# Rounding of theta and of the second slices of k and q: which engine takes which step

## The chip, the cores and the metric

The kernel runs on one core of a Trainium2 chip. The metric is the device time of one execution in microseconds (us), and the figure for a kernel is the median over its runs. A core has a matrix engine, TensorE (PE in the profile, with PEld for its weight loads), and three engines that matter here beside it: VectorE (DVE), ScalarE (ACT) and the queue of SyncE (SP), which issues the transfers. Each engine works through its own list of instructions strictly in order; an instruction that waits holds up everything behind it on its engine.

## The reference

Two stages in a row. The first is a polysketch attention over 4 batches, 4 heads, 1088 positions and head size 32, with a sketch of r = 8. The second is a token mixer with a phase. The reference is in numpy, float32 for the activations.

```python
def phi(x):                                   # r*r = 64 features of a row
    a = einsum('rd,bhsd->bhsr', S1, x)
    b = einsum('rd,bhsd->bhsr', S2, x)
    return einsum('bhsi,bhsj->bhsij', a, b).reshape(..., r * r)
q_p, k_p = phi(q), phi(k)
kv = einsum('bhsf,bhsd->bhfd', k_p, v)
z = sum(k_p, axis=2)
num = einsum('bhsf,bhfd->bhsd', q_p, kv)
den = einsum('bhsf,bhf->bhs', q_p, z)[..., None] + 1e-06
x = num / den                                 # then (B,H,S,D) -> (B,S,128)

theta = x @ w_theta
zr, zi = x * cos(theta), x * sin(theta)
y = einsum('ts,bsd->btd', w_tok_r, zr) + einsum('ts,bsd->btd', w_tok_i, zi)
u = x + y
return u + maximum(u @ w_ch, 0)
```

The denominator can come close to zero, so the kernel computes `den` far more exactly than float32 allows in one go. It does that by cutting the numbers into slices: a value is rounded to a coarse grid, the rest is rounded to a finer grid, and so on, each slice short enough for exact products in float16 matmuls.

## The kernel before, in words

Positions are padded to 9 chunks of 128. For each batch `b` there are these steps.

- `keys_slices(b)`: k is scaled on ACT into `kx` (128x1152, float32) and cut into three float16 slices in `ks`: slot 1 is the first (coarsest) slice, slot 2 the second, slot 0 the rest. Before the change, slot 2 holds the second slice at 2^12 times its value, and a fourth tile, `half`, holds the same slice at its own scale.
- `query_slices(b)`: q is transposed on PE, scaled on ACT into `qx`, and cut into three float16 slices `sl[0]` to `sl[2]` (tiles q0, q1, q2).
- `matrices(b)`: `keys_sums` multiplies the key slices with each other on PE (lines 306 and 308), `keys_matrix` cuts the sums again into four levels with many small DVE instructions and makes `mv[b]`, the matrix for the denominators.
- `keys_values(b)`: the 64 features of k and their sum with v.
- `features(b)`: 27 float16 matmuls of the query slices with `mv[b]` (lines 446 to 448), copied by ACT into `lv` (line 449).
- `denominators(b)`: some 25 DVE instructions that put `lv` together into the exact reciprocal `rd` of the denominators. They use `fl` (levels put together), `s` (rounded parts), `pr` (products) and `dn` (sums).
- `queries(b, g)` for g = 0, 1, 2 (three chunks each): features of q (`qp`), numerators `num` on PE (line 519), `x` = num times `rd` on DVE, transposes (line 534), theta on PE (line 539), the rounding of theta to whole turns (lines 543 and 544), Abs and two Sin on ACT (lines 545 to 547), and the products `zr`, `zi` on DVE.
- `mixing(b)`: the large part, line 566: 17 slices of `wT` for each of three column groups of up to 384, two PE instructions each, 408 over the four batches; then the channel step and the output (lines 575 to 587).

At the start the token weights arrive as raw float64 bits in 34 pieces. `load_f32` turns each piece into float32 with three ACT instructions (lines 134 to 136) and two DVE instructions (lines 137 and 138).

The order on every engine is not written out by hand: the Tile framework lays it out at build time from priorities and its own cost estimates. The kernel sets five levels of priority, in this order: "first" (all of batch 0 up to its attention), "weights", "out", "attention" (keys and attention of batches 1 to 3) and "mixing". Within a level, earlier code comes first, but a later instruction whose inputs are there may be put into a gap. The program order is: everything of batch 0, `keys(1)`, `attention(1)`, `keys(2)`, `mixing(0)`, `attention(2)`, `keys(3)`, `mixing(1)`, `attention(3)`, `mixing(2)`, `mixing(3)`.

Buffers are shared by tag. Tag `r` has one buffer, used by `big` in `keys_slices`, by `big` in `query_slices` and by `s` in `denominators`. Tag `q2` has one buffer, used by the third query slice and by `half` of the keys. Tag `qx` has one, used by `kx` and `qx`. Tile `tn` is `n_`, tile `tt` is `t_`. The PSUM pool for tag `w` has three buffers, which `features`, `queries`, `query_slices` and `keys_values` share.

The helpers `ts`, `tt` and `stt` issue DVE instructions, with one tensor input and constants (profile line 97), with two tensor inputs (line 93), and with two tensors and a scalar (line 100).

## Time and profile before

| what | value |
|---|---|
| median of 8 runs | 358.92 us (357.41 to 360.18) |
| the profiled execution | 357.59 us |
| its span, first to last instruction | 355.8 us |
| mean granted TensorE clock | 0.882 |
| PE busy | 272.5 us, 77% |
| DVE busy | 250.4 us, 70% |
| ACT busy | 153.5 us, 43% |
| largest group: line 566 on PE, 384 instructions | 135.1 us |

The profile is of one execution. Its first page gives the busy time of each engine, then the span in 40 slices of 8.9 us each with a busy digit for each engine (9 is 90% or more, 0 is under 10%) and the granted clock of TensorE in tenths. Then come the groups of instructions: line, engine, operation, output and input tile, shape, count, then busy time and mean nanoseconds of one, then the idle time of the engine just ahead of them and what ended it. The time line lists instructions in order of start, with their duration and the idle time ahead of them in brackets. The table by stretches gives busy times of all engines and the clock in chosen windows.

### The profile page before, as it was taken

What the parts mean: (1) busy time and instruction counts of PE and PEld (TensorE: products, weight loads), DVE (VectorE), ACT (ScalarE), POOL (GpSimd) and SP (SyncE); (2) the same over time, 40 slices, a digit from 0 to 9 for tenths busy, and PEclk for the clock granted to TensorE, in tenths of its full rate; (3) what the DMA queues carried; (4) which work ended last, traced back from release to release, by engine and by line L of the source; (5) the groups of instructions that cost most, each with busy time, mean ns of one, the idle gap of its engine ahead of it and who ended that gap; (6) DMA issues with size and microseconds to landing.
All of it is one profiled execution on the core that took longest, in us unless ns stands there. A gap on an engine that the chain in (4) does not pass through costs nothing.

```text
span 355.8 us, 4021 instructions
## 1 busy us (share of the span) xinstructions
PE 272.5 (77%) x1355; PEld 191.0 (54%) x1355; DVE 250.4 (70%) x713; ACT 153.5 (43%) x313; POOL 0.7 (0%) x6
## 2 busy tenths in 40 slices
PE   0406580143527999999589999996999999999994
PEld 0304480021425776766267676674777767766662
DVE  4897886977997599569848793996589479532111
ACT  1799729999765451061233513212345131332000
POOL 0000000000000000000000000000000000000000
PEclk9999955558555899999879999997899999999998
DMA  8668537885520012020100222000000000000010
GB/s 298 225 214 277 170 123 254 301 292 171 177 63 3 0 67 68 0 67 3 44 18 2 66 66 90 1 22 20 0 0 3 0 21 3 22 20 0 3 41 18
DMA packets 11604, 28.78 MB, mean 81 GB/s; under 512 B 1216, under 2 KB 5568, under 8 KB 11584
## 3 DMA queue, kind: packets, MB, share of 16 engines
q1 hardware_dynamic: 11376, 28.51, 24.3%
q8 instruction: 10, 0.16, 0.2%
q14 instruction: 10, 0.08, 0.1%
q10 hardware_dynamic: 208, 0.02, 0.0%
HBM read 26.30 MB, written 2.23 MB: 80 GB/s over the span
## 4 chain that ended last, share of the span: by engine, by line
PE 69%; DVE 17%; ACT 10%; DMA 2%; issue 1%; ACTq 0%
PE y L566 37%; PE w L519 4%; PE acc L398 3%; ACT step L135 3%; ACT step L136 3%; PE w L539 2%; PE y L576 2%; PE y L398 2%; DVE wT L93 2%; PE w L513 2%; PE w L388 2%; PE w L446 2%; PE acc L306 2%; DMA s_t_st<-s_t 2%; ACT wT L134 1%; PE w L447 1%
## 5 line engine op out<-in xcount | busy, mean ns | idle before, releaser
L566 PE MATMUL y<-wT,zst 128*128 128x384 f32 (+1 forms) x384 | 135.1, 481 | 1.4 <-DVE zst L93 1.4
L566 PEld LDWEIGHTS y<-wT,zst 128*128 128x128 f32 x384 | 68.2, 193 | 30.8 <-DVE zst L93 2.3
L585 ACT COPY ot<-y 128x384 f32<-128x384 f32 (+2 forms) x16 | 6.0, 399 | 62.0 <-PE y L580 62.0
L135 ACT ACTIVATE step<-st 128x544 f16<-128x544 f32 (+1 forms) x35 | 27.8, 795 | 4.4 <-DVE wT L93 4.3
L93 DVE CUSTOM_DVE_ANT_0 wT<-wT,step 128x1088 uint16<-128x1088 uint16 x34 | 24.3, 714 | 5.8 <-ACT step L136 5.8
L519 PEld LDWEIGHTS w<-kvbd,qpT 128*128 128x128 f32 x144 | 21.6, 213 | 11.0 <-ACT qpT L517 10.0
L136 ACT ACTIVATE step<-st 128x544 int16<-128x544 uint32 (+1 forms) x35 | 27.4, 783 | 0.0
L519 PE MATMUL w<-kvbd,qpT 128*128 128x64 f32 x144 | 23.3, 296 | 3.0 <-ACT qpT L517 2.9
L134 ACT ACTIVATE wT<-st 128x544 f32<-128x544 f32 x34 | 22.9, 683 | 2.0 <-DMA st<-w_tok 2.0
L517 ACT COPY qpT<-w 128x256 f32<-128x256 f32 x36 | 12.8, 368 | 24.8 <-PE w L513 24.8
L513 PE MATMUL w<-ident,qp 128*128 128x128 f32 x72 | 14.6, 304 | 7.8 <-DVE qp L93 7.7
L93 DVE TENSOR_TENSOR uT<-xT,y 128x384 f32<-128x384 f32 (+1 forms) x12 | 6.3, 527 | 19.2 <-PE y L566 19.1
L97 DVE TENSOR_SCALAR tn<-w 128x384 f32<-128x384 f32 x12 | 6.7, 557 | 18.3 <-PE w L539 18.3
L536 ACT COPY xT<-w 128x384 f32<-128x384 f32 x12 | 5.7, 476 | 29.8 <-PE w L534 29.8
L449 ACT COPY lv<-w 128x384 f32<-128x384 f32 x36 | 14.6, 506 | 6.7 <-PE w L448 6.6
L513 PEld LDWEIGHTS w<-ident,qp 128*128 128x128 f32 x72 | 10.1, 170 | 9.6 <-ACT wT L134 7.9
L97 DVE TENSOR_SCALAR wT<-wT 128x544 int32<-128x544 int32 x34 | 14.5, 431 | 0.0
L398 PEld LDWEIGHTS acc<-ld_v,kp 128*128 128x128 f32 x108 | 13.0, 192 | 1.5
L539 PEld LDWEIGHTS w<-w,xT 128*128 128x128 f32 x72 | 10.8, 217 | 5.3 <-ACT xT L536 4.5
L446 PE MATMUL w<-mv,q 128*128 128x384 f16 x36 | 12.6, 351 | 0.8 <-DVE mv L93 0.8
L404 ACT COPY kvbd<-acc 64x64 f32<-64x64 f32 x6 | 1.2, 207 | 27.6 <-PE acc L398 27.6
L539 PE MATMUL w<-w,xT 128*128 128x128 f32 x72 | 12.0, 309 | 1.0 <-ACT xT L536 1.0
(230 smaller groups left out, 511.0 us busy)
## 6 DMA issues: line engine op xcount, KB each, us to landing
st<-w_tok SPq DMA_DIRECT2D x34, 544.0 KB, 4.7
ld_k<-k_l SPq DMA_DIRECT2D x4, 576.0 KB, 3.8
ld_q<-q_l SPq DMA_DIRECT2D x4, 576.0 KB, 4.2
ld_v<-v_l SPq DMA_DIRECT2D x4, 576.0 KB, 4.0
out<-ot SPq DMA_DIRECT2D x8, 192.0 KB, 2.1
out<-ot SPq DMA_DIRECT2D x4, 128.0 KB, 1.8
st<-w_sq SPq DMA_DIRECT2D x1, 256.0 KB, 4.9
out<-ot SPq DMA_DIRECT2D x4, 32.0 KB, 1.8
```

The costliest lines, as they stand in the source:

```text
L93: eng.tensor_tensor(out=o, in0=a, in1=b, op=op)
L97: V.tensor_scalar(out=o, in0=a, scalar1=s1, scalar2=s2, op0=op0, **kw)
L134: A.activation(dst, hi.bitcast(F32), AF.Copy, scale=2.0**-112)
L135: A.activation(step[:, :, 1].bitcast(F16), hi.bitcast(F32), AF.Copy, scale=2.0**-60)
L136: A.activation(step[:, :, 0], lo.bitcast(U32), AF.Copy, scale=2.0**-29)
L398: nc.tensor.matmul(kv[:, n], kp[:, i * H + 2 * n:i * H + 2 * n + 2].rearrange("p h i j -> p (h i j)"), vn[:, c, 2 * n:2 * n + 2].rearrange ...
L446: nc.tensor.matmul(lp, q0, flat[:, 0:4 * W], start=True, stop=False, skip_group_check=True)
L449: A.copy(lv[:, :, :, c].rearrange("p l t n -> p (l t) n"), lp.rearrange("p (x n) -> p x n", n=HR))
L513: nc.tensor.transpose(tr[:, n * P:(n + 1) * P], qp[:, i * H + 2 * n:i * H + 2 * n + 2].rearrange("p h i j -> p (h i j)"), ident)
L519: nc.tensor.matmul(num[:, i * P + n * 2 * D:i * P + (n + 1) * 2 * D], qpT[:, n], kvbd[b][:, n], start=True, stop=True)
L539: nc.tensor.matmul(th[:, i * P:(i + 1) * P], xT[:, i * P:(i + 1) * P], w2[:, 0], start=True, stop=True)
L566: nc.tensor.matmul(yp[:, :t1 - t0], z, wT[:, i, t0:t1], start=(i == 0), stop=(i == NK - 1))
```

## The change

Four edits.

1. In `keys_slices` the second slice is rounded at its own scale (constant 1.5 x 2^23 x 2^-12) straight into slot 2, without `big` and `half`. What is left is found with a plain subtraction, and ACT multiplies it by 2^12 into slot 0. `keys_sums` and `keys_matrix` follow: slot 2 takes the place of `half`, and two factors 2^-12 become 1.
2. In `query_slices` the second slice is rounded at its own scale into a new float16 tile `half`; ACT multiplies it by 2^10 into `sl[1]`; the rest is subtracted, and ACT multiplies it by 2^10 into `sl[2]`. `big` goes.
3. In `denominators` the fourth row of `fl`, which nobody read, goes with its instruction, and two of the three sums in `dn` become one reduction.
4. In `queries` the first half of the rounding of theta (adding the large constant) goes to ACT; DVE then subtracts the constant and theta in one instruction. The sign of the result is turned, so the sine's scale gets a minus.

```diff
@@ keys_slices
-        big = work.tile([P, NC * P], F32, tag="r", name="r", bufs=1)
         ts(ks[:, 1], kx, ROUND, ALU.add, ROUND, ALU.subtract)
         tt(V, kx, kx, ks[:, 1], ALU.subtract)
-        ts(big, kx, 2.0**12, ALU.mult, ROUND, ALU.add)
-        ts(ks[:, 2], big, ROUND, ALU.subtract)
-        stt(ks[:, 0], kx, 2.0**12, ks[:, 2], ALU.mult, ALU.subtract)
-        half = work.tile([P, NC * P], F16, tag="q2", name="half", bufs=1)
-        A.activation(half, ks[:, 2], AF.Copy, scale=2.0**-12)
-        tiles["ks", b] = ks, half
+        ts(ks[:, 2], kx, ROUND * 2.0**-12, ALU.add, ROUND * 2.0**-12, ALU.subtract)
+        tt(V, kx, kx, ks[:, 2], ALU.subtract)
+        A.activation(ks[:, 0], kx, AF.Copy, scale=2.0**12)
+        tiles["ks", b] = ks
@@ keys_sums, keys_matrix
-            nc.tensor.matmul(gp[:, 0:4:3], half[:, cs], ks[:, 0:3:2, cs],
+            nc.tensor.matmul(gp[:, 0:4:3], ks[:, 2, cs], ks[:, 0:3:2, cs],
...
-             [(x[:, 2], 2.0**-12), (x[:, 3], 2.0**-12), (x[:, 0], 2.0**-12)], *SUM, near=2)
+             [(x[:, 2], 1.0), (x[:, 3], 1.0), (x[:, 0], 2.0**-12)], *SUM, near=2)
@@ query_slices
+        half = work.tile([P, NC * P], F16, tag="half", name="half", bufs=1)
...
-        big = work.tile([P, NC * P], F32, tag="r", name="r", bufs=1)
-        ts(big, qx, 2.0**10, ALU.mult, 1.5 * 2.0**22, ALU.add)
-        ts(sl[1], big, 1.5 * 2.0**22, ALU.subtract)
-        stt(sl[2], qx, 2.0**10, sl[1], ALU.mult, ALU.subtract)
+        ts(half, qx, 1.5 * 2.0**12, ALU.add, 1.5 * 2.0**12, ALU.subtract)
+        A.activation(sl[1], half, AF.Copy, scale=2.0**10)
+        tt(V, qx, qx, half, ALU.subtract)
+        A.activation(sl[2], qx, AF.Copy, scale=2.0**10)
@@ denominators
-        fl = work.tile([P, 4, NT], F32, tag="fl", name="fl", bufs=1)
-        stt(fl[:, 0:3], lv[:, 1], 2.0**-10, lv[:, 0], ALU.mult, ALU.add)
+        fl = work.tile([P, 3, NT], F32, tag="fl", name="fl", bufs=1)
+        stt(fl, lv[:, 1], 2.0**-10, lv[:, 0], ALU.mult, ALU.add)
...
-        stt(fl[:, 3], lv[:, 2, 2], 2.0**-20, fl[:, 2], ALU.mult, ALU.add)
...
-        for j, j0, j1 in ((1, 1, 3), (2, 3, 6)):
-            V.tensor_reduce(out=dn[:, j], in_=pr[:, j0:j1].rearrange("p j (n r) -> p n j r", r=R),
-                            axis=AX.XY, op=ALU.add)
+        V.tensor_reduce(out=dn[:, 1], in_=pr[:, 1:6].rearrange("p j (n r) -> p n j r", r=R), axis=AX.XY, op=ALU.add)
...
-        tt(V, dn[:, 0], dn[:, 0], dn[:, 2], ALU.add)
@@ queries
-        ts(n_, th, ROUND, ALU.add, ROUND, ALU.subtract)
-        tt(V, t_, th, n_, ALU.subtract)
+        A.activation(n_, th, AF.Copy, bias=ROUND)
+        stt(t_, n_, ROUND, th, ALU.subtract, ALU.subtract)
         A.activation(n_, t_, AF.Abs)
         A.activation(n_, n_, AF.Sin, bias=halfpi, scale=-TWO_PI)
-        A.activation(t_, t_, AF.Sin, scale=TWO_PI)
+        A.activation(t_, t_, AF.Sin, scale=-TWO_PI)
```

## The prediction

> **What bounds the kernel now.** I read the 40 slices first, then tables by stretches, then the DVE time line where PE stands idle.

> ```profile
> PE   0406580143527999999589999996999999999994
> DVE  4897886977997599569848793996589479532111
> ACT  1799729999765451061233513212345131332000
> PEclk9999955558555899999879999997899999999998
> ```

> Up to slice 12 (113 us) PE is mostly idle, at half clock, while DVE and ACT turn weights into float32 and take batch 0 through its attention. From 113 us on PE is full: 56.75 of 57 us in 113 to 170, 57.61 of 58 in 182 to 240, 91.52 of 92 in 250 to 342. Work taken off DVE or ACT there is worth nothing by itself. Two dents are left, digits 5 and 6:

> ```profile
> 170.00:172.00 2.00, 1.35 (x6) 0.50 (x4) 1.86 (x5) 0.00 (x0) 0.00 (x0) 1.00 0.00 0
> 172.00:174.00 2.00, 0.98 (x3) 0.30 (x2) 2.00 (x4) 0.48 (x1) 0.00 (x0) 1.00 0.22 62
> 174.00:176.00 2.00, 0.55 (x3) 0.31 (x3) 2.00 (x7) 0.48 (x1) 0.00 (x0) 0.99 0.13 36
> 176.00:178.00 2.00, 1.44 (x2) 0.50 (x2) 1.25 (x5) 1.16 (x1) 0.00 (x0) 0.50 0.34 98
> 242.00:244.00 2.00, 0.59 (x4) 0.28 (x3) 1.92 (x5) 0.79 (x3) 0.00 (x0) 1.00 0.00 0
> ```

> After the length come PE, PEld, DVE, ACT, POOL, then the clock. PE loses 4.4 us in 170 to 180 (and 0.4 in 186 to 188) and 3.1 us in 240 to 246 (0.2 later), while DVE is full; its clock then falls to 0.50 for some 7 us each time. What DVE does there:

> ```profile
> 158.09 1.06 DVE L100 SCALAR_TENSOR_TENSOR fl<-lv 128x864 f32<-128x864 f32 x1 [2.07 <-ACT lv L449]
> ...
> 174.88 0.75 DVE L97 TENSOR_SCALAR r<-kx 128x1152 f32<-128x1152 f32 x1
> ...
> 176.05 0.75 DVE L97 TENSOR_SCALAR ksl<-r 128x1152 f16<-128x1152 f32 x1
> ...
> 178.25 1.30 DVE L100 SCALAR_TENSOR_TENSOR ksl<-kx,ksl 128x1152 f16<-128x1152 f32 x1
> 179.46 0.18 DVE L93 TENSOR_TENSOR rd<-rd,gm 128x36 f32<-128x36 f32 x1
> 179.68 0.56 DVE L93 TENSOR_TENSOR x<-w,rd 128x384 f32<-128x384 f32 x1
> ```

> mixing(0) is done at 170, and mixing(1) needs batch 1's z, which needs x, which needs rd. Between the steps of denominators(1) stand three large instructions of keys_slices(2), for the next batch. They come so late although kx, less its first slice, stood ready at 155.9: big shares buffer r with s, and s is read until 168.6. The second dent is the same: r<-kx at 241.21, ksl at 242.59 and 243.55, x at 244.99, with that kx ready at 227.9. In the third attention (x at 304.55) PE has mixing work and loses nothing.

> **The change, part by part.** Durations come from the profiled execution, 357.59 us (span 355.8 and 1.8 around it), 1.33 under the median 358.92. I add savings and put the sum on the median; neighbours on DVE overlap by some 0.08 us, so sums of durations are slightly large.

> ```profile
> L97 DVE TENSOR_SCALAR tn<-w 128x384 f32<-128x384 f32 x12 | 6.7, 557 | 18.3 <-PE w L539 18.3
> L536 ACT COPY xT<-w 128x384 f32<-128x384 f32 x12 | 5.7, 476 | 29.8 <-PE w L534 29.8
> L295 ACT ACTIVATE half<-ksl 128x1152 f16<-128x1152 f16 x4 | 4.7, 1164 | 1.1 <-DVE ksl L97 1.1
> L93 DVE TENSOR_TENSOR kx<-kx,ksl 128x1152 f32<-128x1152 f32 x4 | 5.4, 1348 | 0.0
> L100 DVE SCALAR_TENSOR_TENSOR ksl<-kx,ksl 128x1152 f16<-128x1152 f32 x4 | 5.3, 1322 | 0.0
> ```

> Keys, per batch on DVE: 0.75 + 0.75 + 1.32 go, 0.75 + 1.35 come: 0.72 saved. ACT keeps one 1.16 us instruction, now at the end of the chain: the last slice comes at 0.75 + 1.35 + 0.75 + 1.35 + 1.16 = 5.36 us instead of 4.92. Buffer r is no longer needed, so the second rounding need not wait for s.

> Queries, per batch: DVE 0.75 + 0.76 + 1.35 go, 0.76 + 1.36 come: 0.74 saved. ACT gains two instructions of 128x1152, 2.33 us; chain again 0.4 longer. In batches 1 to 3 mv is later than the slices (features(1) starts at 152.6, right after mv at 151.88; slices done at 135.9), which hides that.

> Denominators, per batch: the dropped row 0.45 and one addition 0.19 go. The reductions of 0.74 and 1.04 become one over 1440 elements; the slope between 576 and 864 elements gives 1.65, so 0.13 goes. Together 0.77, all ahead of rd.

> Theta, 12 times: 0.56 goes from DVE. ACT's Copy with a constant isn't in the trace; bounds are 0.48 (Copy from PSUM) and 0.57 (scaling by a pointer, line 426). I take 0.48, the same shape without a pointer. The two-tensor instruction stays near 0.55 (uT<-y,uT: 0.554). In the dents DVE had waited 3.4 and 3.7 us for theta, so the step changes engine at no loss, 0 to 0.1 us; elsewhere PE is full, which hides it. No table load is added: Copy, Abs and Sin already follow each other after 112 us with no further load.

> Matmuls and transfers stay as they are, and no issue on SP or POOL moves. In all DVE loses 15.6 us (4 x (0.72 + 0.74 + 0.77) + 12 x 0.56) and ACT gains 15.1 (4 x 2.33 + 12 x 0.48). Where ACT's new instructions wait, line 449's lv copies, qpT and xT copies stand behind them, and PE waits for those. Only four places of that reach the end.

> Start: queries(0) frees 0.74 just ahead of kp at 44.56, which PE's kv matmuls wait for; then ACT converts weights without a pause from 54 to 77. Denominators(0) frees 0.77 in 83 to 102.7. Against it, theta's first step queues on ACT behind weight conversions: in 104.7 to 108.7 ACT is taken, while DVE did that step at 106.90; bounds 0 and 1.6. I take 0.5 of it: **1.0 us earlier** (bounds 2.2 earlier, and later by 1.6 + 2.33 - 1.5 = 2.4 if the two new q instructions also delay conversions).

> Ahead of features(1): in 113 to 152 DVE is freed of 0.72 + 0.74 + 3 x 0.56 = 3.1 us. The chain to mv(1) is one of small instructions that often wait for PE (0.95 for line 338, 0.59 for 344, 0.75 for 355), so a third of it: **1.0** (bounds 0 and 3.1).

> First dent: 0.77 surely. The keys give 0.72 if they stay in place, or all 2.8 if rounding and subtraction move into the 2.07 us of DVE idle ahead of 158.09. I take **2.0 in all** (bounds 1.5 and 3.6). With the 1.0 before it, that stays under the 4.8 us that PE loses there.

> Second dent: scaled kx is ready only at 225.4, after the lv chain has begun, so 0.77 + 0.72 = **1.5** (bounds 0, if other work fills the place, and 3.3, all that PE loses there).

> Sum: 1.0 + 1.0 + 2.0 + 1.5 = 5.5; 358.9 - 5.5 = **353.4**.

> [...]

> **Rivals.** (a) More than that: both dents close (4.8 + 3.3) and the start gains 2.2: 348.6, and PE's half clock goes with them: it is busy at 0.50 in 180 to 182.5 and 246 to 250.7, 7.2 us that would take 3.6: 345. For it: DVE is the only engine full in the dents. Against: kx in the second comes late.

> (b) Slower: the order. With r free, work for the next batch is ready earlier and fills small gaps ahead of x. Rounding and subtraction of batch 3 already stand between two steps of denominators(2), at 225.73 and 226.52. If the query slices of the next batch, freed from waiting for kx in buffer qx, come ahead of x, each dent takes 4.22 us and gives back 1.5: 358.9 - 1.0 + 2 x 2.7 = 363.3. It decides if these slices stand before x on DVE in both dents; in one alone it makes about 359. Against: batch 2's q transposes run at 198.5, 19 us after kx was released, so something else, I suppose the three PSUM buffers w that queries(1) occupies, holds them.

> (c) No change: what moves up refills both dents, and only the start's 1.0 is left: 357.9. For it: DVE always has a backlog in the dents. Against: the backlog's largest piece, 2.8 us, can go into idle time.

> **How the numbers follow.** Forecast 0.45, (a) 0.15, (c) 0.15, (b) 0.25. A measurement of this kernel can tell about 0.5%, 1.8 us, from no change. Faster than 357.1: 0.60; within: 0.16 (c and the near end of b); slower than 360.7: 0.24. With every bound at its good end (the two before the first dent capped at its 4.8) the sum is 2.2 + 4.8 + 3.3 = 10.3, with every one at its bad end 2.4 later and 1.5 earlier: 348.6 to 359.8. Not all go one way, so the forecast's own range is 350 to 357. The range 346.5 to 362 takes in most of (a) and (b) up to half-way between one dent and two (359 to 363).

> **What would show it.** Right: no r<-kx between dn and x; PE idle in the dents down from 4.8 to 2 and from 3.3 to 2; DVE busy near 235 us, ACT near 169; x of batch 0 before 102. Wrong: q slices or cm ahead of x in a dent; first mixing matmul after 113; theta's Copy waiting behind conversions or lv copies for over 1 us.

## The result and the profile after

The changed kernel takes 353.67 us (median of 11 runs, 352.53 to 355.94). The kernel before, in runs on the same chips, takes 358.78 us (median of 32). The ratio is 0.9864, with a 95% interval of 0.9839 to 0.9889: 1.4% faster. The forecast said 353.4. The total fits, but the terms behind it do not, and most of this part is about that.

The profiled execution of the changed kernel took 352.29 us, with a span of 350.5 us and a mean granted clock of 0.895 (before: 357.59, 355.8, 0.882). Both profiles are from the quick end of their kernel's runs: the four longest of the changed kernel (355.2 to 355.9 us, clock 0.875 to 0.880) have, by an estimate from clock and span, 11 to 15 us more of half clock than the profiled one, and no trace shows where it lies in them. DVE is busy for 237.8 us (250.4 before), ACT for 166.8 us (153.5 before). The 40 slices, in the order of the rows shown of before:

```profile
PE   0406790026136799999978999999999999999994
DVE  4897867885998169657997685986768299332111
ACT  0799849999955457033214376023555410442000
PEclk9999955558555599999999999999999999999998
```

One dent is left, digits 7 and 8 in slices 20 and 21 (counted from 0); the second is gone, and the clock row stays at 9 from the start's end up to the last slice. Stretches of 2 us in the two places (after the length come PE, PEld, DVE, ACT, POOL, then the clock):

```profile
178.00:180.00 2.00, 1.36 (x6) 0.50 (x4) 2.00 (x4) 0.48 (x1) 0.00 (x0) 1.00 0.00 0
180.00:182.00 2.00, 0.93 (x3) 0.40 (x3) 2.00 (x9) 0.00 (x0) 0.00 (x0) 1.00 0.31 98
182.00:184.00 2.00, 1.27 (x7) 0.92 (x8) 1.97 (x7) 0.61 (x2) 0.00 (x0) 1.00 0.00 0
242.00:244.00 2.00, 2.00 (x16) 1.79 (x15) 0.39 (x3) 0.60 (x2) 0.00 (x0) 1.00 0.04 8
```

PE still loses time with DVE full at 178 to 184, and none at 242. The two places as a whole, first before, then after:

```profile
160.00:190.00 30.00, 25.23 (x117) 16.11 (x117) 23.98 (x49) 6.97 (x16) 0.00 (x0) 0.89 0.07 19
240.00:262.00 22.00, 18.69 (x101) 13.38 (x100) 14.58 (x40) 7.46 (x17) 0.00 (x0) 0.84 0.03 8
```

```profile
160.00:190.00 30.00, 26.08 (x128) 16.94 (x127) 28.09 (x62) 7.47 (x18) 0.00 (x0) 1.00 0.06 19
240.00:262.00 22.00, 22.00 (x142) 16.79 (x141) 14.30 (x50) 11.16 (x26) 0.00 (x0) 1.00 0.03 9
```

PE's idle time falls from 4.77 to 3.92 us in the first and from 3.31 to 0 in the second, and the clock is 1.00 in both.

**A sum that closes.** For each kernel I add up tables of 2 us stretches from 130 us on. Time after 130 us is PE's work left there at full clock (busy time times clock), plus PE's idle time, plus what is lost because busy PE had less than full clock. (PE's pace does go with the clock in the trace of before: the matmul behind one of line 306, 128x384, starts 0.32 us after it at a clock of 0.50, 247.75 to 248.07, and 0.16 us after it at 1.00, 252.46 to 252.62.) Before: 130 + 206.8 + 13.3 + 5.7 = 355.8. After: 130 + 211.2 + 9.3 + 0 = 350.5. So, from one profile each, the start got worse by up to 4.4 us, idle time fell by 4.0, and 5.7 of half clock went. (The whole work of PE, the same in all kernels, comes out between 250 and 254 us by this method, so a term of work left is good to about 2 us. The other two do not depend on it. Before and after come out at 251.7 and 252.9; by what is lost ahead of 130 us, 85.1 and 88.3, the start got worse by 3.2.)

**Where keys_slices(2) went.** DVE in the first dent's run-up, after:

```profile
160.18 1.06 DVE L100 SCALAR_TENSOR_TENSOR fl<-lv 128x864 f32<-128x864 f32 x1 [3.24 <-ACT lv L447]
161.15 0.75 DVE L97 TENSOR_SCALAR ksl<-kx 128x1152 f16<-128x1152 f32 x1
162.48 1.35 DVE L93 TENSOR_TENSOR kx<-kx,ksl 128x1152 f32<-128x1152 f32 x1
163.86 0.76 DVE L97 TENSOR_SCALAR ksl<-kx 128x1152 f16<-128x1152 f32 x1
164.66 1.35 DVE L93 TENSOR_TENSOR kx<-kx,ksl 128x1152 f32<-128x1152 f32 x1
165.93 0.57 DVE L97 TENSOR_SCALAR s<-fl,dgr 128x576 f32<-128x576 f32 x1
...
182.37 0.18 DVE L93 TENSOR_TENSOR rd<-rd,gm 128x36 f32<-128x36 f32 x1
182.68 0.55 DVE L93 TENSOR_TENSOR x<-w,rd 128x384 f32<-128x384 f32 x1
```

The three large instructions that stood just ahead of rd are gone from there, as forecast. But they did not go into DVE's idle time ahead of fl, which grew to 3.24 us. All four, 4.2 us of work, now stand between fl and s: s starts 5.75 us after fl, before 2.50 (158.09 to 160.59). With fl itself 2.1 us later, x comes at 182.68 us, later than before (179.68). PE loses less all the same, because mixing(0) now lasts until 178 us instead of 170. It began 3.6 us later (116.89 against 113.25), and other work, keys_sums(2) among it, now lies within it: DVE takes up its result, `cm` of batch 2, at 175.50 us, before at 186.02. That these two are why PE loses less fits the trace; no run changes them alone.

### The profile page after: what moved, and what is told of

Same layout as the page of the kernel before. It is cut to its first block, busy times and chain, and to the rows that moved or that the text cites. A ratio compares the mean times of both kernels' runs of the same rounds, so it can differ in the third digit from the quotient of the medians.

```text
span 350.5 us, 4014 instructions
## 1 busy us (share of the span) xinstructions
PE 268.7 (77%) x1355; PEld 189.0 (54%) x1355; DVE 237.8 (68%) x681; ACT 166.8 (48%) x333; POOL 0.7 (0%) x6
## 4 chain that ended last, share of the span: by engine, by line
PE 62%; DVE 17%; ACT 14%; DMA 4%; issue 1%; ACTq 0%; SPq 0%
PE y L560 31%; PE w L513 5%; ACT step L135 4%; ACT step L136 3%; PE acc L395 3%; PE w L533 3%; PE y L395 2%; PE w L507 2%; ACT lv L447 2%; ACT wT L134 2%; PE y L570 2%; PE w L385 2%; DMA s_t_st<-s_t 2%; DVE kx L93 1%; PE acc L303 1%
## 5 line engine op out<-in xcount | busy, mean ns | idle before, releaser
L560 PE MATMUL y<-wT,zst 128*128 128x384 f32 (+1 forms) x384 | 133.6, 478 | 2.0 <-DVE zst L93 1.9
L93 DVE CUSTOM_DVE_ANT_0 wT<-wT,step 128x1088 uint16<-128x1088 uint16 x34 | 24.4, 717 | 4.5 <-ACT step L136 3.8
L93 DVE TENSOR_TENSOR uT<-xT,y 128x384 f32<-128x384 f32 (+1 forms) x12 | 6.3, 528 | 22.5 <-PE y L560 22.5
L100 DVE SCALAR_TENSOR_TENSOR tt<-tn,w 128x384 f32<-128x384 f32 x12 | 6.6, 552 | 15.1 <-ACT tn L537 15.1
L97 DVE TENSOR_SCALAR wT<-wT 128x544 int32<-128x544 int32 x34 | 14.5, 432 | 1.4 <-ACT wT L134 1.4
L93 DVE TENSOR_TENSOR kp<-ks 128x768 f32<-128x768 f32 x12 | 11.4, 950 | 4.5 <-PE acc L395 2.5
L93 DVE TENSOR_TENSOR zst<-x,tn 128x384 f32<-128x384 f32 (+1 forms) x12 | 6.1, 511 | 11.3 <-ACT tn L540 11.3
L444 PE MATMUL w<-mv,q 128*128 128x384 f16 x36 | 12.6, 351 | 0.9 <-DVE mv L93 0.9
L533 PEld LDWEIGHTS w<-w,xT 128*128 128x128 f32 x72 | 10.6, 214 | 5.0 <-ACT xT L530 4.4
```

The costliest lines, as they stand in the source:

```text
L93: eng.tensor_tensor(out=o, in0=a, in1=b, op=op)
L97: V.tensor_scalar(out=o, in0=a, scalar1=s1, scalar2=s2, op0=op0, **kw)
L533: nc.tensor.matmul(th[:, i * P:(i + 1) * P], xT[:, i * P:(i + 1) * P], w2[:, 0], start=True, stop=True)
L560: nc.tensor.matmul(yp[:, :t1 - t0], z, wT[:, i, t0:t1], start=(i == 0), stop=(i == NK - 1))
```

## The start: 1 us gained, then given back

At 48 us the forecast gain is there: DVE's kp, which PE's kv matmuls wait for, starts at 47.57 us, before at 48.60. Then it turns. keys_matrix(0) cuts `cm` with a chain of small DVE instructions, among the weights' conversions. Its last one (cz) before, and the next conversion behind it:

```profile
52.84 0.22 DVE L97 TENSOR_SCALAR cz<-cut_z 128x128 f16<-128x128 f32 x1
55.58 0.72 DVE L93 CUSTOM_DVE_ANT_0 wT<-wT,step 128x1088 uint16<-128x1088 uint16 x1 [2.52 <-ACT step L136]
```

After, the same wait stands in the middle of the chain, and the last cz comes 3.67 us later:

```profile
51.09 0.28 DVE L100 SCALAR_TENSOR_TENSOR cut_r<-cm,cut_r 128x128 f32<-128x128 f32 x1
53.90 0.72 DVE L93 CUSTOM_DVE_ANT_0 wT<-wT,step 128x1088 uint16<-128x1088 uint16 x1 [2.52 <-ACT step L136]
54.54 0.28 DVE L100 SCALAR_TENSOR_TENSOR cut_r<-cm,cut_r 128x128 f32<-128x128 f32 x1
...
56.51 0.22 DVE L97 TENSOR_SCALAR cz<-cut_z 128x128 f16<-128x128 f32 x1
```

The wait is for ACT, and ACT itself stands in its order behind a copy that waits 2.47 us for PE:

```profile
49.33 0.82 ACT L135 ACTIVATE step<-st 128x544 f16<-128x544 f32 x1 [1.88 <-DVE wT L93]
52.62 0.42 ACT L401 COPY kvbd<-y 64x64 f32<-64x64 f32 x2 [2.47 <-PE y L395]
53.06 0.81 ACT L136 ACTIVATE step<-st 128x544 int16<-128x544 uint32 x1
```

So a small step of batch 0's chain waits for a conversion, which waits for another step of batch 0. One more weight piece is then converted ahead of features(0) (26 step conversions on ACT instead of 25), and features(0) starts at 78.79 us instead of 76.88, x of batch 0 at 105.15 instead of 102.68. The copy of theta on ACT is not what delays the start here: it begins at 109.44 us, when theta's matmul ends. Abs and the sines behind it stand after qpT copies that wait for PE (1.64 and 1.26 us, at 111.88 and 113.94).

## The experiments

The table gives medians, the ratio to the kernel before, and from one profile each the span and the three terms of the sum above. Each ratio is against the kernel before as measured along with that kernel (medians 358.78 to 359.95 us), so kernels are best compared by ratio. A profile need not be of a typical run: those of changed, t_alone and d_alone are of their quickest run (d_alone's is 2.8 us under its median), those of no_k and keys_out of their slowest.

| kernel | us | ratio, 95% interval | span | work left at 130 us | idle after | clock |
|---|---|---|---|---|---|---|
| before | 358.78 | 1 | 355.8 | 206.8 | 13.3 | 5.7 |
| changed | 353.67 | 0.9864 [0.9839, 0.9889] | 350.5 | 211.2 | 9.3 | 0.0 |
| k_alone | 360.71 | 1.0013 [0.9974, 1.0051] | 358.9 | 209.6 | 11.9 | 7.4 |
| q_alone | 360.87 | 1.0051 [1.0023, 1.0079] | 358.6 | 209.6 | 13.9 | 5.1 |
| t_alone | 357.79 | 0.9955 [0.9930, 0.9979] | 355.0 | 208.7 | 13.5 | 2.8 |
| d_alone | 357.18 | 0.9943 [0.9914, 0.9972] | 352.6 | 207.4 | 12.1 | 3.1 |
| own_r | 355.22 | 0.9898 [0.9856, 0.9940] | 353.4 | 208.4 | 10.6 | 4.4 |
| no_k | 356.78 | 0.9930 [0.9903, 0.9958] | 356.5 | 213.0 | 10.8 | 2.6 |
| no_q | 347.96 | 0.9683 [0.9651, 0.9714] | 346.0 | 209.4 | 6.7 | 0.0 |
| no_t | 347.73 | 0.9691 [0.9658, 0.9725] | 345.7 | 209.7 | 6.0 | 0.0 |
| kq0_back | 346.24 | 0.9633 [0.9598, 0.9669] | 345.0 | 208.3 | 6.7 | 0.0 |
| kqt0_back | 356.77 | 0.9930 [0.9902, 0.9958] | 354.6 | 208.7 | 9.9 | 6.0 |
| own_td | 346.50 | 0.9662 [0.9627, 0.9697] | 345.2 | 207.8 | 7.4 | 0.0 |
| keys_out | 350.20 | 0.9732 [0.9685, 0.9780] | 349.0 | 212.2 | 6.8 | 0.0 |

**The four edits one by one.** Each is done alone on the kernel before. First the keys' edit:

```diff
 k_alone: keys_slices, keys_sums, keys_matrix as changed
-        big = work.tile([P, NC * P], F32, tag="r", name="r", bufs=1)
...
+        ts(ks[:, 2], kx, ROUND * 2.0**-12, ALU.add, ROUND * 2.0**-12, ALU.subtract)
+        tt(V, kx, kx, ks[:, 2], ALU.subtract)
+        A.activation(ks[:, 0], kx, AF.Copy, scale=2.0**12)
```

> Only the edit of the keys, on the kernel before. Theory A (work and waits taken off DVE ahead of x, with the half clock as the second part): the second rounding no longer waits for s, so the three large key instructions leave the place just ahead of x(1) and x(2); both dents shrink from 4.8 and 3.3 us of idle PE to 3 or less, and if they no longer fall under half clock, PE saves up to 5 us on top: 352 to 356 us, first mixing matmul at 113 as before. Theory B (the order does it, not the work): what the keys free is filled by other work of the next batch, both dents stay over 3 us with their 6.8 us of half clock each: 357.5 to 360 us.

No change can be told (1.0013), and the gain that theory A expected did not come. The order did change: the key instructions stand ahead of fl, at 158.86 us, but fl comes only at 163.37 and x at 183.25. features(0) is 3.3 us later, at 80.21, again with 26 conversions ahead of it.

```diff
 q_alone: query_slices as changed
-        ts(big, qx, 2.0**10, ALU.mult, 1.5 * 2.0**22, ALU.add)
...
+        ts(half, qx, 1.5 * 2.0**12, ALU.add, 1.5 * 2.0**12, ALU.subtract)
+        A.activation(sl[1], half, AF.Copy, scale=2.0**10)
+        tt(V, qx, qx, half, ALU.subtract)
+        A.activation(sl[2], qx, AF.Copy, scale=2.0**10)
```

> Only the edit of the query slices, on the kernel before. The later start of the changed kernel (first mixing matmul at 116.9 instead of 113.2 us) is either its doing or theta's. Theory A: the two new ACT instructions of batch 0 (2.3 us at 42 to 45 us) push weight conversions back, features(0) starts near 78.8 instead of 76.9, the first mixing matmul near 115, and the dents stay: 359.5 to 361.5 us. The forecast's own step said 0.5 us gained at the start: 358 us.

0.5% slower, just resolved: features(0) at 80.41 us, and the dents as before, since the keys still share r with s.

```diff
 t_alone: theta as changed
-        ts(n_, th, ROUND, ALU.add, ROUND, ALU.subtract)
-        tt(V, t_, th, n_, ALU.subtract)
+        A.activation(n_, th, AF.Copy, bias=ROUND)
+        stt(t_, n_, ROUND, th, ALU.subtract, ALU.subtract)
```

> Only the edit of theta, on the kernel before. Theory A: features(0) at 76.9 as before, x(0) at 102.7, then theta's first step waits on ACT behind weight conversions: first mixing matmul 1 to 2 us later than 113.2; the dents keep their idle time and half clock: 359 to 361 us. If theta's share of DVE work (1.7 us a batch) shortens the chain to features(1), the first dent shrinks by 1 to 2 us and the total is the same or less: 356 to 358.5 us.

0.45% faster, where 0 to 2 us of loss was the first expectation. The start is untouched (features(0) at 76.9, first mixing matmul at 113.4 us, before 113.25). The feared wait at theta(0) does not show in this kernel.

```diff
 d_alone: denominators as changed
-        stt(fl[:, 3], lv[:, 2, 2], 2.0**-20, fl[:, 2], ALU.mult, ALU.add)
...
+        V.tensor_reduce(out=dn[:, 1], in_=pr[:, 1:6].rearrange("p j (n r) -> p n j r", r=R), axis=AX.XY, op=ALU.add)
```

> Only the edit of the denominators, on the kernel before: one row of fl, one addition and one reduction fewer, about 0.77 us of DVE in each batch ahead of rd. Theory A, as in the forecast: x comes 0.7 us earlier at the start and in each of the two dents, half clock unchanged: 356 to 357.5 us. If other work fills the place: 358.5 to 359.5 us.

0.57% faster, 2 us for 0.77 us less in each chain. The four ratios multiplied give 1.0013 x 1.0051 x 0.9955 x 0.9943 = 0.9962. The whole change is 0.9864, so the edits do not add up; something arises only when they are together.

**The shared buffer alone.** This kernel keeps every operation of the kernel before and only gives `big` of the keys a buffer of its own:

```diff
 own_r
-        big = work.tile([P, NC * P], F32, tag="r", name="r", bufs=1)
+        big = work.tile([P, NC * P], F32, tag="rk", name="rk", bufs=1)
```

> The kernel before, but the intermediate of the keys' second slice has a buffer of its own instead of sharing r with s. DVE work is unchanged. Theory A with the shared buffer as the cause: the key instructions move ahead of or between the steps of denominators as in the changed kernel, PE idle in the first dent falls by 1 to 3 us: 353 to 357 us. If the 0.7 us of DVE work saved per batch is what counts, or the order, nothing is gained: 358 to 360 us.

1.0% faster with no instruction less. keys_slices(2) now runs ahead of fl (159.42 us), and `cm` of batch 2 is at 162.5 instead of 186.0 us. mv(2) is written by 201.4, before by 218.7 us, so features(2) starts at 210.41 instead of 218.72. The changed kernel shows nearly the same: cm at 175.5, mv(2) by 201.8, features(2) at 210.63. In own_r PE loses nothing from 230 to 262 us, so the buffer alone closes the second dent. What goes with it is not a shorter chain ahead of its x, but batch 2's `cm` coming 10 us and more sooner. The first dent keeps 3.9 us of idle time and its half clock, though the keys stand ahead of fl. features(2), which followed right upon mv(2) before, now has 9 us to spare there.

**Each edit left out of the change.** The diffs are against the changed kernel. The question is what each edit gives in the company of the others.

```diff
 no_k: keys as before
+        big = work.tile([P, NC * P], F32, tag="r", name="r", bufs=1)
...
+        stt(ks[:, 0], kx, 2.0**12, ks[:, 2], ALU.mult, ALU.subtract)
+        A.activation(half, ks[:, 2], AF.Copy, scale=2.0**-12)
```

> The changed kernel without the keys' edit, so that the keys share buffer r with s again. Theory A: r<-kx and the two after it stand ahead of x in both dents again; both dents over 3 us and both with 6.8 us of half clock: 357 to 360 us. If theta, queries and denominators carry the gain by themselves: 353 to 355 us.

```diff
 no_q: queries as before
-        ts(half, qx, 1.5 * 2.0**12, ALU.add, 1.5 * 2.0**12, ALU.subtract)
...
+        ts(big, qx, 2.0**10, ALU.mult, 1.5 * 2.0**22, ALU.add)
```

> The changed kernel without the queries' edit. Theory A: the query slices aren't in the dents and cost 1 to 3 us at the start, so leaving the edit out gives 351 to 353.5 us. If the keys' edit alone fixes the later start, nothing changes: 353 to 354.5 us. If q's buffer (big in r) holds the next denominators back, it is slower: 355 to 357 us.

```diff
 no_t: theta as before
-        A.activation(n_, th, AF.Copy, bias=ROUND)
-        stt(t_, n_, ROUND, th, ALU.subtract, ALU.subtract)
+        ts(n_, th, ROUND, ALU.add, ROUND, ALU.subtract)
+        tt(V, t_, th, n_, ALU.subtract)
```

> The changed kernel without the edit of theta. Theory A: theta alone took the half clock out of the second dent and left the start as it was; without it the second dent may come back: 353.5 to 357 us. If the keys' and denominators' edits close the second dent by themselves, theta is worth nothing here: 352 to 354 us.

Without the keys' edit 0.9930, just short of the 357 to 360 us expected: it is the one that the change needs. Without the queries' edit 0.9683 and without theta's 0.9691: either makes the kernel 1.7 to 1.8% faster than the whole change, though each puts 3 to 7 us back on DVE. In both, the four key instructions run ahead of fl (from 156.76 and from 155.32 us), x comes at 178.46 and 176.99 us, and no half clock is left after the start. None of the expectations on record for these two foresaw a gain of that size. So the busy time that an edit saves does not tell what it is worth, and theta's edit, a gain alone, is a loss here.

**Batch 0 as before.** To separate the start from the rest, only batch 0's keys and queries go back to the old steps; batches 1 to 3 keep all edits.

```diff
 kq0_back (the same in query_slices)
+        if b:
             ts(ks[:, 2], kx, ROUND * 2.0**-12, ALU.add, ROUND * 2.0**-12, ALU.subtract)
...
+        else:
+            ts(big, kx, 2.0**12, ALU.mult, ROUND, ALU.add)
...
```

> The changed kernel, with batch 0's key and query slices cut as before (batches 1 to 3 as changed). The keys' edit alone and the queries' edit alone each put one more weight piece on ACT and DVE ahead of features(0) (26 conversions instead of 25) and brought the first mixing matmul to 117.0 and 116.2 us. Theory A: with both undone for batch 0 the start is as before, first mixing matmul at 113 to 113.6 us, and the gains in the dents stay: 349 to 351 us. Theory B (every edit shuffles the order everywhere): start earlier, but the first dent comes back with its half clock: 353 to 357 us.

346.24 us, the lowest median here and under both expected ranges. 25 conversions stand ahead of features(0) again (77.34 us), and the work left at 130 us is 208.3, 2.9 less than in the changed kernel. The start is not back as before, though: x(0) comes at 105.06 and the first mixing matmul at 117.47 us. And 2.6 us of idle time went too, all of it in the first dent. DVE in this kernel:

```profile
154.59 0.76 DVE L97 TENSOR_SCALAR ksl<-kx 128x1152 f16<-128x1152 f32 x1 [0.46 <-ACT kx L285]
...
157.69 1.36 DVE L93 TENSOR_TENSOR kx<-kx,ksl 128x1152 f32<-128x1152 f32 x1
159.06 1.06 DVE L100 SCALAR_TENSOR_TENSOR fl<-lv 128x864 f32<-128x864 f32 x1
...
176.45 0.55 DVE L93 TENSOR_TENSOR x<-w,rd 128x384 f32<-128x384 f32 x1
```

The keys fill the wait for lv, nothing large stands between fl and s, and x comes 17.4 us after fl; in the changed kernel it takes 22.5.

```diff
 kqt0_back, against kq0_back
+        if b:
             A.activation(n_, th, AF.Copy, bias=ROUND)
             stt(t_, n_, ROUND, th, ALU.subtract, ALU.subtract)
+        else:
+            ts(n_, th, ROUND, ALU.add, ROUND, ALU.subtract)
+            tt(V, t_, th, n_, ALU.subtract)
```

> The changed kernel with batch 0's keys, queries and theta as before. With keys and queries of batch 0 undone features(0) was back at 77.3, but the first mixing matmul stayed at 117.5, because theta's steps on ACT stand behind qpT copies that wait for PE. Theory A: with theta of batch 0 on DVE the first mixing matmul comes at 113 to 114.5, the loss before 130 us falls from 86.8 to 85 to 86: 344 to 346 us. If the order on ACT isn't theta's doing, the same as without it: 346 to 347 us.

This puts three more instructions of 0.5 us of batch 0 back, and costs 10.5 us (346.24 to 356.77). Expected were 344 to 347 us. The work left at 130 us hardly differs (208.7 and 208.3), and the first mixing matmul comes at 116.35 us instead of 117.47, not at the 113 to 114.5 of the theory, so theta(0) explains little of the start. But the order at fl has flipped, and PE gets a half clock of 13.65 us in the dent:

```profile
159.86 1.06 DVE L100 SCALAR_TENSOR_TENSOR fl<-lv 128x864 f32<-128x864 f32 x1 [3.24 <-ACT lv L464]
160.84 0.75 DVE L97 TENSOR_SCALAR ksl<-kx 128x1152 f16<-128x1152 f32 x1
...
182.25 0.55 DVE L93 TENSOR_TENSOR x<-w,rd 128x384 f32<-128x384 f32 x1
```

**The free buffer with the two cheap edits.** The kernel before with a buffer of its own for `big`, and the edits of theta and of the denominators; no rescaling on ACT.

```diff
 own_td
-        big = work.tile([P, NC * P], F32, tag="r", name="r", bufs=1)
+        big = work.tile([P, NC * P], F32, tag="rk", name="rk", bufs=1)
...
+        A.activation(n_, th, AF.Copy, bias=ROUND)
...
+        V.tensor_reduce(out=dn[:, 1], in_=pr[:, 1:6].rearrange("p j (n r) -> p n j r", r=R), axis=AX.XY, op=ALU.add)
```

> The kernel before with a buffer of its own for the intermediate of the keys' second slice, and with the edits of theta and of the denominators, but keys and queries cut as before. If the gain of the keys' edit is the freed buffer r alone, the losses of PE after 130 us (idle time and half clock, with the tail's 5) fall from 19 to 7 to 9 us as in the kernels with the keys' edit, and the start stays at 85 us of loss: 344 to 348 us. If the keys' edit matters by its own instructions (0.7 us less DVE a batch, 5.4 us of chain ending on ACT), the dents keep 12 us or more of loss: 351 to 355 us.

346.50 us: as fast as kq0_back within the intervals, without the edits' rescalings on ACT. Keys ahead of fl (155.29 us), x at 178.06, 25 conversions ahead of features(0), but the first mixing matmul only at 117.69. no_q differs from it in having the keys' edit in place of the free buffer, and the intervals of the two overlap (0.9662 and 0.9683). So what the keys' edit brings can be had from a free buffer, without the work that it takes off DVE.

own_r has the same free buffer and gains 1.0%, here it is 3.4%. From fl to x it takes 19.1 us in own_r and 19.9 in k_alone, and 17.2 to 17.6 in own_td, kq0_back, no_q and no_t, which have the edit of the denominators besides. Of the kernels so far only these four have under 2.2 us of idle time in the first dent, and no half clock. So the keys' place ahead of fl is not enough by itself; no run has just it and the denominators' edit.

**The order by itself.** What goes with the keys standing behind fl? In the changed kernel ACT scales kx piece by piece between the copies of lv, and the last quarter of kx is ready only when lv is:

```profile
155.25 0.54 ACT L285 ACTIVATE kx<-ld_k,ipk 128x288 f32<-128x288 f32 x1
155.69 1.23 ACT L447 COPY lv<-w 128x384 f32<-128x384 f32 x3
156.79 0.56 ACT L285 ACTIVATE kx<-ld_k,ipk 128x288 f32<-128x288 f32 x1
...
159.27 0.87 ACT L447 COPY lv<-w 128x384 f32<-128x384 f32 x2
160.00 0.57 ACT L285 ACTIVATE kx<-ld_k,ipk 128x288 f32<-128x288 f32 x1
```

The last kernel is the changed one with keys_slices(2) raised to the level "out", above the attention. No operation changes.

```diff
 keys_out
-        keys_slices(b)
+        with level("out" if b == 2 else "attention"): keys_slices(b)
```

> The changed kernel with one line altered: keys_slices(2), the slices of batch 2's keys, is issued at level out instead of attention. No operation changes. In the built order of the VectorE the four large instructions of keys_slices(2) now stand ahead of denominators(1)'s first step (fl from lv), where in the changed kernel they stand behind it; up to that place the order is as in the changed kernel but for a few small ones. Theory of the order (what is worth 6 to 7 us between the changed kernel and the one with batch 0's keys and queries as before is this one place, not what batch 0 does): the four instructions run in the 3.2 us that VectorE waits there, fl starts by 160.5, first x of batch 1 at 177 to 179 instead of 182.7, PE's loss after 130 us falls from 9.3 to 6 to 7.5, and the time from 353.7 to 350 to 352 us, since the start keeps its loss of about 88; its start would have to be better by 2 to reach 347. Rival (the place is only a companion of batch 0's later start; the chain into mixing(1) is set by PE and ScalarE): x at 181 or later, 353 to 355 us. Third theory (moving the keys ahead delays fl as in the kernel with the keys' edit alone, where fl came at 163.4 and x at 183.3): fl after 162.5, 354 to 358 us.

```profile
156.24 1.81 ACT L285 ACTIVATE kx<-ld_k,ipk 128x288 f32<-128x288 f32 x4
158.07 0.21 ACT L401 COPY kvbd<-acc 64x64 f32<-64x64 f32 x1
158.31 3.54 ACT L447 COPY lv<-w 128x384 f32<-128x384 f32 x9
```

```profile
158.08 0.76 DVE L97 TENSOR_SCALAR ksl<-kx 128x1152 f16<-128x1152 f32 x1 [0.75 <-ACT kx L285]
...
162.34 1.05 DVE L100 SCALAR_TENSOR_TENSOR fl<-lv 128x864 f32<-128x864 f32 x1
...
179.90 0.55 DVE L93 TENSOR_TENSOR x<-w,rd 128x384 f32<-128x384 f32 x1
```

ACT now scales kx in one go, and the keys stand ahead of fl. The time falls to 350.20 us, inside the 350 to 352 of the order theory, and the loss after 130 us from 9.3 to 6.8, as it said. In the first dent PE's idle time (165 to 200 us) falls from 3.9 to 1.2 us. Two of its numbers were missed: fl starts at 162.34 instead of 160.5, since kx was only ready at 158.08, and x at 179.90 instead of 177 to 179. fl is 2.2 us later than in the changed kernel and x still 2.8 us earlier, 17.6 us after fl. So the order alone is worth something: 3.5 us by the medians, 4.7 by the ratios (the intervals don't meet), but 1.5 by the two profiles, the changed kernel's quickest run and this one's slowest. That it is one place alone is not shown. The same line moved the keys of batch 3 (first at 218.28 us, in the changed kernel at 232.35) and the first mixing matmul (119.29, in the changed kernel 116.89). The other 4 us between this kernel and kq0_back agree with the start: 212.2 against 208.3 us of work left at 130 us, with equal idle time after it.

## Why the prediction was right, and where it was not

The forecast's sum was 5.5 us of gain; the profiles differ by 5.3. Term by term, from one profile each:

| term | forecast | measured |
|---|---|---|
| start and ahead of features(1) | 2.0 gained | up to 4.4 lost (work left at 130 us) |
| first dent, idle | 2.0 gained | 0.85 gained |
| second dent, idle | 1.5 gained | 3.3 gained |
| half clock in both dents | 0 | 5.7 gained |
| rest | 0 | 0.15 lost |

- **The start was the wrong sign.** The gain ahead of kp was right (1.03 us by the trace, 0.74 forecast). The step that failed is the bound on what stands against it: I let ACT's added instructions delay conversions one for one, at most 2.4 us in all. What happened was a new wait in the middle of a chain that I had not listed, keys_matrix(0), and then one more weight piece ahead of features(0). k_alone and q_alone show that either slice edit alone brings the extra piece; kq0_back shows that both undone for batch 0 take it away. But the piece is only part of the later start: kq0_back and own_td have 25 pieces as before, and their first mixing matmul comes at 117.47 and 117.69 us all the same. t_alone, d_alone and own_r start it at 113.4 to 114.8, so some combination of edits delays it. Which one, and how, stays open.
- **Ahead of features(1)** a gain of 1.0 was forecast; it starts 1.7 us later (154.31 against 152.62), with the start's loss in it.
- **First dent.** Right that the keys would leave the place ahead of rd once r was free. Wrong in where they went: I had taken the two places "stays" and "into the idle time ahead of fl" as the ends, and the keys went to a third, between fl and s. It put s 3.3 us further behind fl, and x came later than before. The prediction had seen that place in use, with the keys of batch 3 between two steps of denominators(2) at 225.73 us, and did not count with it here. The upper end, keys in the idle time, is what kq0_back, no_q, no_t and own_td show.
- **Second dent.** The term was mis-sized because it used the wrong lever. I counted the shorter chain (1.5). The runs show that the freed buffer moves the keys of batch 2, and with them mv(2) by 17 us and features(2) by 8 (own_r). k_alone, whose queries still use r, has the keys early and features(2) at 222.73 all the same; why is open.
- **The half clock.** The forecast gave it nothing and left 3.6 us to rival (a). The sum over the stretches makes it 5.7 us. The 3.6 counted only PE's 7.2 us of busy time behind the dents; within the half clock PE is busy for 11.5 us in all. In these profiles it was the largest single gain, and it came with the shorter dents, as in rival (a).
- **Rivals.** (a) was right on the second dent and on the clock, and wrong on the first dent, which kept 3.9 us, and on the start. The order was the right thing to fear, but (b) named the wrong instructions: not the next batch's query slices but its keys, in an earlier place of the chain. (c) did not happen.
- **The signs.** Of those named for right, r<-kx did leave the place ahead of x and the second dent closed, but the first kept 3.9 us of idle time and x of batch 0 came at 105.15 us. Of those named for wrong, two came: `cm` ahead of x in the first dent (175.50 us), and the first mixing matmul at 116.89. By its own signs the mechanism was half right.
- **DVE's work.** 12.6 us went instead of 15.6, and ACT gained 13.3 instead of 15.1. On DVE most of it is the overlap that the prediction names: 32 instructions fewer at 0.08 us (kx<-kx,ksl at 164.66 in the rows of after runs 1.35 us, s starts at 165.93) are 2.6, by an estimate.
- **Sizes of instructions** were right. ACT's step of theta is 492 ns (0.48 forecast), the merged reduction 1645 ns (1.65), the rescalings 1.16 to 1.17 us:

```profile
L537 ACT ACTIVATE tn<-w 128x384 f32<-128x384 f32 x12 | 5.9, 492 | 14.9 <-PE w L533 14.9
L483 DVE TENSOR_REDUCE dn<-lv 128x36 f32<-128x1440 f32 x4 | 6.6, 1645 | 0.0
L430 ACT ACTIVATE q<-half 128x1152 f16<-128x1152 f16 x4 | 4.7, 1168 | 0.0
L432 ACT ACTIVATE q<-qx 128x1152 f16<-128x1152 f32 x4 | 4.7, 1162 | 0.0
```

So the total was right by luck: errors of both signs, up to 6.4 us too hopeful up to 130 us and 6.2 too cautious after it, cancelled. Each was larger than the half width of the range that the forecast gave itself (350 to 357).

## What to carry to other kernels

When an order is laid out by priorities, a freed buffer or a moved step shifts work for several batches; ask for each large instruction that becomes free earlier into which gap it will go, and what stands right behind that gap. Four instructions stood ahead of a wait in kq0_back and behind it in kqt0_back, and that came with 10.5 us; taking 12.6 us of work off DVE came with 5.1. Try the pieces of a change one at a time and left out one at a time: here the buffer with two cheap edits was as good as anything, and the edits of the queries and of theta were each a loss in the company of the other three.

## What the runs showed of the hardware

```profile
244.00:246.00 2.00, 0.88 (x4) 0.88 (x4) 1.53 (x4) 0.80 (x1) 0.00 (x0) 0.56 0.30 82
```

```profile
242.00:244.00 2.00, 1.00 (x3) 0.30 (x2) 1.88 (x5) 0.00 (x0) 0.00 (x0) 1.00 0.00 0
244.00:246.00 2.00, 0.55 (x3) 0.38 (x4) 2.00 (x5) 1.23 (x3) 0.00 (x0) 1.00 0.00 0
```

The first drops to half clock at 244.2 us, the second not at all: its clock is 1.00 in every stretch from 184 to 352 us. Laid on the grid of its own trace, the idle time falls differently. In the kernels with two bounds the steps are counted from a change of their own clock, and the busy time is bounded by an estimate from the tables of 2 us stretches:

| kernel | grid step, us | PE busy in it, of 3.41 us | clock in the next step |
|---|---|---|---|
| before | 172.55 to 175.97 | 1.46 | 0.50 |
| before | 240.82 to 244.23 | 1.35 | 0.50 |
| changed | 177.67 to 181.08 | 1.82 | 1.00 |
| t_alone | 240.97 to 244.39 | 2.0 to 2.4 | 1.00 |
| t_alone | 244.39 to 247.80 | 1.5 to 2.1 | 1.00 |
| own_td | 174.65 to 178.07 | 2.0 to 2.4 | 1.00 |
| k_alone | 178.00 to 181.41 | 2.0 to 2.3 | 0.50 |
| own_r | 183.47 to 186.88 | 2.0 to 3.1 | 0.50 |

In before 2.06 us of the idle time lie in one step; in t_alone it is spread over two. But PE's busy time in a step does not tell the clock of the next by itself: k_alone, with at least 2.0 us, went to half clock, and the changed kernel, with 1.82, did not. What decides it was not shown; no run shifted the idle time alone.
